# Attention output: rows loaded and stored by one transfer each, and weight blocks made in chosen slots

## The chip, the cores and the metric

The kernel runs on one core of one Trainium2 chip. The metric is device time in microseconds (us), from start to end of one execution; the median of several executions is compared. The core has a matrix engine (TensorE, PE in the profile, with its weight loads as PEld), three engines for elementwise work (VectorE = DVE, ScalarE = ACT, GpSimd = POOL), and SyncE (SP), which here does nothing but issue transfers (DMAs). All of them run their own instructions in order and wait for each other by semaphores. Transfers issued by any of them run on the core's 16 DMA engines.

## The reference

Two independent computations, put side by side in one output of 2048 rows and 2 x 576 columns.

```
A (attention):  q, k, v = x@wq, x@wk, x@wv        S = 2048 rows, D = 576, H = 32 heads of 18
  for each of 4 segments of 512 rows, for each head:
    p     = softmax(q k^T * scale + causal mask)
    a_mem = phi(q) M / (phi(q) z + 1e-6)           M, z: sums over earlier segments of phi(k)^T v, phi(k)
    o     = g * a_mem + (1 - g) * p v              g = sigmoid(beta), one number for each head
  out[:, :576] = concat_heads(o) @ wo
B (Fourier mixing):  out[:, 576:] = Cr @ (x @ Hr^T) - Ci @ (x @ Hi^T)     Cr, Ci: 2048 x 2048
```

Matrix products are made from numbers split into a high part (rounded to the matrix engine's float32 mode) and a low part (the rest): hi*hi + hi*lo + lo*hi.

## The kernel before, in words

**Stages.** First q, k, v and the memory of all segments are projected (up to some 225 us). Then the attention and the Fourier part B run interleaved (up to 938 us). Last stands the output stage, the product of the attention's result with `wo`.

**Attention.** `attention()` (L1110) is written as slots: 68 steps p of 8 slots each, one step for one pair of heads in one segment, with later work of earlier pairs in the same slots (scores for maxima in step p, second scores two and three steps later, the product with v four steps later: `F_LAG`, `T_LAG`, `V_LAG`). The main loop (L1181) takes one slot after the other, and behind each slot as many pieces of part B (`dense()`) as keep both at the same share of their work. `later(n, fn)` puts a call n slots ahead; transfers and low parts are mostly issued so. So the order on each engine is the order in which these lines run; no scheduler moves anything.

**The result on its way.** The normalised result of four heads is turned by VectorE (`turn_out`, L1081) and written to DRAM, to `od[s]`, four feature blocks of 128 x 512 rows for each segment s. Feature columns beyond 512 (64 of the 576) are gathered in `TAILS`, turned by `turn_tails` (L1096) and written to `odt[s]`, 256 rows of 128: twice for each segment, so eight times.

**The output stage.** The 16 tiles of 128 rows are taken as 8 pairs (tile n and tile n + 8), and each pair's product with `wo` is made by a Strassen-like scheme of seven products (`p1` to `p7` in `output_stage`, L849) in place of eight: rows in two halves (the two tiles), columns in two halves of 288, features in two halves of 256; features beyond 512 are added by `tail` terms. A product is 6 or 8 matmuls of 128 x 288 (`seventh`, L832), 50 for a pair. For this each pair's rows are loaded (`o_load`, `o_pair`, L684), split and combined into sums and differences (`left`, L789; the first pair's differences on VectorE, later ones on VectorE and GpSimd), two pairs ahead of their use at most. PSUM banks for the products alternate; `p6`, `p4` and `p7` of one pair share one bank, so `p7` waits until VectorE has emptied `p6` (L864).

Loading one tile takes three transfers: 128 x 4 x 128 from `od`, and twice 64 x 128 from `odt` (the same tail for the upper and the lower half of the partitions). Storing one tile takes four transfers of 32 rows (`store`, L843), because `turn_out` leaves the rows of a segment permuted in groups of 32. In the last pair some stores go on ScalarE's queue.

**Weight blocks.** `right_operands()` (L696) makes what the seven products need of `wo`: for each feature half c, the split blocks B11, B21, B22 (`plain`), the split differences T1 to T4 (`combined`, four differences of 128 x 288 in place, each using the one before, two on GpSimd and two on VectorE in turn, then high parts on ScalarE and low parts on VectorE), and the tail rows (`tails`). It is a generator: from step 60 on it goes one piece further at each slot, and at its end it loads the first pair (step 66) and goes on with `left(0)`. The second pair is loaded in the main loop's last part, once part B has no more chunks waiting.

Before, low parts of plain blocks are made by GpSimd, those of the tails by VectorE, those of the differences by VectorE.

**What sets the order of the transfers.** SyncE issues nearly all of them in program order; a transfer whose source or destination is not ready holds up those behind it. Completion is counted on eight counters that are used in turn, so a transfer also waits for the one that used its counter before.

Of the kernel before, what the change touches and what calls it, by code (L numbers as in the profile page):

```python
# [12 lines left out]
F32 = mybir.dt.float32  # L13
# [27 lines left out]
def infini_attention_and_fnet(ctx: ExitStack, tc: tile.TileContext, xT, wqk, w8, wv, wo, beta, xtT, cT, hT, out):  # L41
# [46 lines left out]
    def later(n, fn, *a):  # L88
        due.setdefault(clock[0] + n, []).append((fn, a))
# [54 lines left out]
    def wide_tile(cols):  # L144
        return lambda: wide.tile([P, cols], F32R, name="wide", tag="wide")
# [538 lines left out]
    def o_load(t, tile_of):  # L684
        s, a = divmod(t, 4)
        o = tile_of()
        dma(o[:, :4], od[s][:, a * P:a * P + P].rearrange("c p x -> p c x"))
        for i in range(2):
            dma(o[64 * i:64 * i + 64, 4], odt[s][64 * a:64 * a + 64])
        O[t] = o  # L690

    def o_pair(n):
        for t in (n, n + 8):
            o_load(t, lambda: sr.tile([P, 5, P], F32, name="craw", bufs=4))

    def right_operands():  # L696
        raw = {}
# [5 lines left out]
        def pause(n):  # L703
            for _ in range(n):
                yield

        def plain(c):
            b11 = wide.tile([P, 2, 288], F32R, name="wide", tag="wide")
            b2 = [wide_tile(D)() for _ in range(2)]
            WO["B11", c] = b11[:, 0], b11[:, 1]  # L710
            WO["B21", c], WO["B22", c] = ((b2[0][:, cs], b2[1][:, cs]) for cs in (slice(0, 288), slice(288, D)))
            for hi, lo, a in ((b11[:, 0], b11[:, 1], raw[c][:, :288]), (b2[0], b2[1], raw[c + 2])):
                act.activation(hi, a, AF.Copy)
                yield
                pool.tensor_tensor(lo, a, hi.bitcast(F32), OP.subtract)
                yield

        def cross(a, b, raw):
            act.activation(a, raw, AF.Copy)
            act.activation(b, raw, AF.Copy)  # L720
            yield
            dve.tensor_tensor(a[:64], raw[:64], a[:64].bitcast(F32), OP.subtract)
            dve.tensor_tensor(b[64:], raw[64:], b[64:].bitcast(F32), OP.subtract)
            yield

        def tails():
            w = [wide_tile(D)() for _ in range(2)]
            d = wide.tile([P, 2, 288], F32R, name="wide", tag="wide")
            TAIL[1], TAIL[2] = ([t[:, cs] for t in w] for cs in (slice(0, 288), slice(288, D)))
            TAIL[0] = [d[:, i] for i in range(2)]  # L730
            r = raw[4]
            yield from cross(*w, r)
            pool.tensor_tensor(r[:, :288], r[:, :288], r[:, 288:], OP.subtract)
            yield
            yield from cross(*TAIL[0], r[:, :288])
# [4 lines left out]
        spare = []  # L740

        def combined(c):
            a, b = raw.pop(c), raw.pop(c + 2)
            b11, b12, b21, b22 = a[:, :288], a[:, 288:], b[:, :288], b[:, 288:]
            if c == 0:
                spare.extend(stage(i, n) for i in range(2) for n in "qk")
                to = [[t[:, :D]] for t in spare]
            else:
                to = [[stage(2, n)[:, :D]] for n in "qk"] + [[wide_tile(D)()], [t[:, D:D + 288] for t in spare[:2]]]
            pool.tensor_tensor(b11, b12, b11, OP.subtract)  # L750
            yield
            dve.tensor_tensor(b12, b22, b12, OP.subtract)
            yield
            pool.tensor_tensor(b22, b22, b11, OP.subtract)
            yield
            dve.tensor_tensor(b21, b21, b22, OP.subtract)
            yield
            for names, r, hi, lo in ((("T1", "T3"), a, *to[:2]), (("T4", "T2"), b, *to[2:])):
                act.activation(hi[0], r, AF.Copy)
                yield  # L760
                at = 0
                for l in lo:
                    w = l.shape[1]
                    dve.tensor_tensor(l, r[:, at:at + w], hi[0][:, at:at + w].bitcast(F32), OP.subtract)
                    at += w
                for i, n in enumerate(names):
                    WO[n, c] = hi[0][:, 288 * i:288 * i + 288], lo[i] if len(lo) > 1 else lo[0][:, 288 * i:288 * i + 288]
                yield

        for k in (0, 2, 4):  # L770
            load(k)
            yield
        yield from pause(5)
        yield from plain(0)
        yield from tails()
        load(1)
        yield from pause(15)
        yield from combined(0)
        load(3)
        yield from pause(3)  # L780
        yield from plain(1)
        yield from combined(1)
        for t in (0, 8):
            o_load(t, lambda: sq.tile([P, 4, 256], F32, name="oraw", tag="qs3" if t else "ks3").rearrange(
                "p a x -> p (a x)")[:, :5 * P].rearrange("p (k x) -> p k x", k=5))
        yield from pause(4)
        yield from left(0)

    def left(n):  # L789
        one, two = O.pop(n), O.pop(n + 8)  # L790
# [50 lines left out]
            pe.matmul(o, a, b, start=first and i == 0, stop=True, skip_group_check=True)  # L841

    def store(t, y, cs, last=False):  # L843
        for q in range(4):
            r = 512 * (t // 4) + P * q + 32 * (t % 4)
            queue = nc.scalar if last and q >= 2 else nc.sync
            queue.dma_start(out[r:r + 32, cs], y[32 * q:32 * q + 32, cs])

    def output_stage():  # L849
        C, Z, U = slice(0, 288), slice(288, 576), {}  # L850
# [393 lines left out]
```

## Time and profile before

| | |
|---|---|
| median of 3 executions | 1009.91 us (1009.61 to 1010.26) |
| the profiled execution | 1010.71 us |
| its span, first to last instruction | 1009.0 us |
| granted TensorE clock, mean | 0.991 |
| TensorE busy | 984.3 us (98%) |
| VectorE, ScalarE, GpSimd busy | 786.2, 714.8, 675.6 us |
| transfers on SyncE's queue (q1) | 305248 packets, 207.15 MB |

In the profile's rows a group of instructions stands with its line, engine, operation and `out<-in` by the program's names, then count, busy time, mean duration in ns, and the idle time of the engine ahead of it with what ended it. Names that matter here: `raw` (rows of wo as loaded), `wide` and `late` (split weight blocks), `oraw`, `craw` (loaded rows of a pair; `craw` also holds part B's chunks), `ls`, `l`, `lb` (sums and parts of the first pair's rows), `u` (finished products, VectorE's and ScalarE's output), `d`, `s`, `t`, `pv` (PSUM banks), `ptt` (transposed probabilities), `og`, `ogt`, `oglt` (attention result and its turned forms). A stretch A:B is a piece of the span in us.

### The profile page before, as it was taken

What the parts mean: (1) busy time and instruction counts of PE and PEld (TensorE: products, weight loads), DVE (VectorE), ACT (ScalarE), POOL (GpSimd) and SP (SyncE); (2) the same over time, 40 slices, a digit from 0 to 9 for tenths busy, and PEclk for the clock granted to TensorE, in tenths of its full rate; (3) what the DMA queues carried; (4) which work ended last, traced back from release to release, by engine and by line L of the source; (5) the groups of instructions that cost most, each with busy time, mean ns of one, the idle gap of its engine ahead of it and who ended that gap; (6) DMA issues with size and microseconds to landing.
All of it is one profiled execution on the core that took longest, in us unless ns stands there. A gap on an engine that the chain in (4) does not pass through costs nothing.

```text
span 1009.0 us, 25590 instructions
## 1 busy us (share of the span) xinstructions
PE 984.3 (98%) x9246; PEld 921.7 (91%) x9246; DVE 786.2 (78%) x2112; ACT 714.8 (71%) x1686; POOL 675.6 (67%) x744
## 2 busy tenths in 40 slices
PE   9999999999999999999999999999999999998895
PEld 8989989899999999999999999999999999888895
DVE  6657667684778877878898887788889889988673
ACT  6757575754877878778878878877777777875341
POOL 2667575775767766766767777667766767786451
PEclk9999999999999999999999999999999999999898
DMA  7638466666778899899999988789999998896464
GB/s 242 198 121 262 149 202 243 216 236 210 170 192 200 235 235 222 210 223 253 224 250 225 223 203 174 185 228 211 244 227 214 238 226 230 218 207 146 124 161 107
DMA packets 305615, 208.92 MB, mean 207 GB/s; under 512 B 206288, under 2 KB 260432, under 8 KB 305488
## 3 DMA queue, kind: packets, MB, share of 16 engines
q1 hardware_dynamic: 305248, 207.15, 80.3%
q8 instruction: 72, 1.18, 0.5%
q14 instruction: 55, 0.45, 0.1%
q10 hardware_dynamic: 240, 0.14, 0.1%
HBM read 121.32 MB, written 57.93 MB: 178 GB/s over the span
## 4 chain that ended last, share of the span: by engine, by line
PE 77%; DVE 7%; ACT 4%; POOL 3%; issue 3%; DMA 3%; SPq 1%; POOLq 0%; DVEq 0%; ACTq 0%
PE d L583 35%; PE s L933 7%; PE v L84 4%; PE pv L1051 4%; PE qk L250 4%; PE d L630 3%; PE d L628 3%; PE d L629 3%; PE pv L1052 2%; DMA craw<-od 2%; PE m L363 1%; PE qk L84 1%; PE t L1007 1%; PE t L841 1%; DVE r L276 1%
## 5 line engine op out<-in xcount | busy, mean ns | idle before, releaser
L939 DVE CUSTOM_DVE_ANT_0 s<-s,causal 128x128 f32<-128x128 f32 (+3 forms) x512 | 248.5, 503 | 95.7 <-PE s L933 86.3
L456 POOL TENSOR_TENSOR clo<-craw,chi 128x512 fp32r<-128x512 f32 x158 | 219.7, 1391 | 88.6 <-ACT chi L451 61.8
L583 PE MATMUL d<-wide,chi 128*128 128x288 f32 x1408 | 263.2, 304 | 1.7 <-DVE y L653 1.7
L583 PEld LDWEIGHTS d<-wide,chi 128*128 128x128 f32 x1408 | 211.9, 190 | 4.2 <-DVE y L653 2.2
L583 PE MATMUL d<-wide,clo 128*128 128x288 f32 x704 | 174.1, 314 | 0.0
L973 POOL TENSOR_TENSOR hl<-pf,hl 128x768 f16<-128x768 f32 x64 | 114.0, 1781 | 68.7 <-ACT hl L969 57.2
L933 PE MATMUL s<-ks,qs 108*128 108x128 bf16 (+3 forms) x512 | 133.0, 303 | 2.9 <-DVE negm L939 1.2
L1019 ACT ACTIVATE phi<-t 128x384 f16<-128x384 f32 x128 | 61.7, 482 | 103.1 <-PE t L1016 103.1
L962 ACT ACTIVATE pf<-s,nb 128x128 f32<-128x128 f32 (+3 forms) x256 | 128.1, 526 | 6.2
L583 PE MATMUL d<-ab,chi 128*128 128x288 f32 x640 | 123.4, 302 | 0.0
L583 PEld LDWEIGHTS d<-wide,clo 128*128 128x128 f32 x704 | 118.5, 190 | 1.5
L1034 DVE TENSOR_TENSOR plo<-pf,phi 128x384 f16<-128x384 f32 (+1 forms) x128 | 118.6, 927 | 0.0
L1020 ACT ACTIVATE pf<-t 128x384 f32<-128x384 f32 (+1 forms) x192 | 99.5, 518 | 6.1 <-PE t L1007 5.7
L451 ACT ACTIVATE chi<-craw 128x512 fp32r<-128x512 f32 x160 | 100.1, 626 | 2.3 <-PE d L583 2.0
L583 PEld LDWEIGHTS d<-ab,chi 128*128 128x128 f32 x640 | 97.9, 189 | 0.5
L969 ACT ACTIVATE hl<-pf 128x768 f16<-128x768 f32 (+1 forms) x128 | 87.4, 730 | 2.0
L583 PE MATMUL d<-ab,clo 128*128 128x288 f32 x320 | 83.1, 309 | 0.0
L628 PE MATMUL d<-wide,chi 128*128 128x288 f32 x256 | 81.5, 318 | 0.0
L630 PE MATMUL d<-wide,clo 128*128 128x288 f32 x256 | 75.7, 296 | 0.9 <-POOL clo L456 0.9
L629 PE MATMUL d<-wide,chi 128*128 128x288 f32 x256 | 75.7, 296 | 0.0
L1034 POOL TENSOR_TENSOR plo<-pf,phi 128x384 f16<-128x384 f32 x64 | 61.8, 965 | 13.8 <-ACT pf L1020 11.0
L973 DVE TENSOR_TENSOR hl<-pf,hl 128x512 f16<-128x512 f32 x64 | 68.8, 1075 | 0.0
(279 smaller groups left out, 2531.4 us busy)
## 6 DMA issues: line engine op xcount, KB each, us to landing
craw<-cT SPq DMA_DIRECT2D x128, 256.0 KB
ks<-kd SPq DMA_DIRECT2D x32, 432.0 KB
qs<-qd SPq DMA_DIRECT2D x32, 432.0 KB
craw<-xtT SPq DMA_DIRECT2D x32, 320.0 KB
vd<-vs SPq DMA_DIRECT2D x16, 440.0 KB
vst<-vd SPq DMA_DIRECT2D x32, 220.0 KB
qd<-p SPq DMA_DIRECT2D x16, 384.0 KB
kd<-p SPq DMA_DIRECT2D x16, 384.0 KB
```

The costliest lines, as they stand in the source:

```text
L451: act.activation(hi, raw[:, :4], AF.Copy)
L456: engine.tensor_tensor(lo, raw[:, :4], hi.bitcast(F32), OP.subtract)
L583: pe.matmul(o[h], a, b[:, h * 288:h * 288 + 288], start=start, stop=stop)
L628: pe.matmul(o, xh[:, k], wl[k][:, cs], start=k == 0, stop=False)
L629: pe.matmul(o, xh[:, k], wh[k][:, cs], start=False, stop=False)
L630: pe.matmul(o, xl[:, k], wh[k][:, cs], start=False, stop=False)
L933: pe.matmul(o[:, c:c + w], q[:, i * P:w], k[:, :w], start=True, stop=True)
L939: dve.tensor_tensor_reduce(o[:, c:c + w], o[:, c:c + w], CAUSAL[0][:, L - w:], scale=scale, scalar=-LOWEST, op0=OP.add, op1=OP.min, accum_ ...
L962: act.activation(f[:, FIRST_COL[i]:FIRST_COL[i] + w], o[:, c:c + w], AF.Exp, bias=nb[:, i:i + 1], scale=-1.0)
L973: engine.tensor_tensor(hl[:, 1, a:b], f[:, a:b], hl[:, 0, a:b], OP.subtract)
L1020: act.activation(f[:, r:r + w], o[:, :w], AF.Exp, bias=LIFT, scale=SCALE)
L1034: (pool if kind == 2 else dve).tensor_tensor(lo[:, a:b], f[:, a:b], hi[:, a:b], OP.subtract)
```

## The change

1. `od[s]` gets a fifth block. When a segment's second tail write is out, three slots later one more transfer copies `odt[s]` into that block, each 64 rows twice (128 KB read, 256 KB written), four times in all. With it `o_load` is one transfer of 128 x 5 x 128.
2. `store` writes a tile with one transfer of 128 rows, the last tile's half with two of 64 rows, one on SyncE and one on ScalarE. The rows of columns 0 to 575 stay in the permuted order in the device's output; the caller puts them in order.
3. The second pair (tiles 1 and 9) is loaded in slot 4 of step 67, into the buffers `phi` and `plo` of the attention, in place of the load after the attention's end. The first pair is loaded in slot 5 of step 66 in place of slot 7.
4. `right_operands` is no generator any more: it writes a plan of calls, each at a step and slot. The plain blocks and tails begin at step 57 in place of 60. The low parts of the tails go from VectorE to GpSimd; the four differences that GpSimd made go to VectorE; the 576-column low parts of T1 to T4 become two of 288 each. For c = 0 the differences stand in step 64 and the low parts in step 65, for c = 1 in steps 66 and 67.
5. `left(0)` begins behind slot 5 of step 67 (before: behind slot 3).

TensorE's instructions and their order are the same in both.

```diff
-    od = [dram.tile([4, 4 * P, P], F32, name=f"od{s}") for s in range(NSEG)]
+    od = [dram.tile([5, 4 * P, P], F32, name=f"od{s}") for s in range(NSEG)]
...
-        dma(o[:, :4], od[s][:, a * P:a * P + P].rearrange("c p x -> p c x"))
-        for i in range(2):
-            dma(o[64 * i:64 * i + 64, 4], odt[s][64 * a:64 * a + 64])
+        dma(o, od[s][:, a * P:a * P + P].rearrange("c p x -> p c x"))
...
+        def at(p, slot, fn, *a):
+            PLAN.setdefault(8 * p + slot, []).append((fn, a))
...
+        def combined_low(c, n):
+            k, names = ((c, ("T1", "T3")), (c + 2, ("T4", "T2")))[n]
+            for i, x in enumerate(names):
+                low(dve, WO[x, c][1], WO[x, c][0], k, (L_, R_)[i])
...
+        at(57, 2, load, 0)
+        at(57, 4, load, 2)
+        at(58, 2, first_block, 0)
+        at(58, 2, second_row, 0)
+        at(58, 2, load, 4)
+        at(58, 4, block_low, 0)
+        at(59, 4, row_low, 0)
+        at(59, 2, tails)
+        at(60, 4, lambda: low(pool, late["w"][0], late["w"][0], 4, rows=lower))
+        at(61, 4, lambda: low(pool, late["w"][1], late["w"][1], 4, rows=upper))
+        at(61, 6, difference, pool, (4, L_), (4, L_), (4, R_))
+        at(62, 2, tail_difference)
+        at(62, 4, lambda: low(pool, TAIL[0][0], TAIL[0][0], 4, L_, lower))
+        at(62, 6, lambda: low(pool, TAIL[0][1], TAIL[0][1], 4, L_, upper))
+        at(62, 6, load, 1)
+        at(63, 6, first_block, 1)
+        at(64, 4, block_low, 1)
+        for c, p in ((0, 64), (1, 66)):
+            a, b = c, c + 2
+            if c:
+                at(65, 6, load, 3)
+                at(66, 2, second_row, 1)
+                at(66, 3, row_low, 1)
+            at(p, 3 + c, difference, dve, (a, L_), (a, R_), (a, L_))
+            at(p, 3 + c, difference, dve, (a, R_), (b, R_), (a, R_))
+            at(p, 5 + c, difference, dve, (b, R_), (b, R_), (a, L_))
+            at(p, 5 + c, difference, dve, (b, L_), (b, L_), (b, R_))
+            for n in range(2):
+                at(p + 1, 2, combined, c, n)
+                at(p + 1, 3 + n, combined_low, c, n)
         for t in (0, 8):
-            o_load(t, lambda: sq.tile(...tag="qs3" if t else "ks3")...)
-        yield from pause(4)
-        yield from left(0)
+            at(66, 5, o_load, t, lambda t=t: sq.tile(...tag="qs3" if t else "ks3")...)
+        for t, tag in ((1, "phi"), (9, "plo")):
+            at(67, 4, o_load, t, lambda tag=tag: sa.tile([P, 5, P], F32, name="oraw", tag=tag, bufs=2))
...
     def store(t, y, cs, last=False):
-        for q in range(4):
-            r = 512 * (t // 4) + P * q + 32 * (t % 4)
-            queue = nc.scalar if last and q >= 2 else nc.sync
-            queue.dma_start(out[r:r + 32, cs], y[32 * q:32 * q + 32, cs])
+        for q in range(2 if last else 1):
+            rows = slice(64 * q, 64 * q + 64) if last else slice(0, P)
+            (nc.scalar if q else nc.sync).dma_start(out[t * P:t * P + P][rows, cs], y[rows, cs])
...
+        if u:
+            later(6, dma, od[s][4].rearrange("(a c r) x -> a c (r x)", a=4, c=2),
+                  odt[s].rearrange("(a c r) x -> a c (r x)", a=4, c=1).to_broadcast([4, 2, 64 * P]))
...
-    ready = right_operands()
+    right_operands()
+    ready = None
     for n, w in enumerate(attention()):
         tick()
         ta += w
-        if n >= 8 * (NP - 4):
+        for fn, a in PLAN.pop(n, ()):
+            fn(*a)
+        if n == 8 * (NP + V_LAG - 1) + 5:
+            ready = left(0)
+        if ready:
             next(ready, None)
...
-        if not c_raw and 1 not in O:
-            o_pair(1)
```

More of the change, by code (lines that the diff above doesn't have):

```diff
@@ L701, in load @@
             dma(raw[k], wo[k])
[L703 to L724, printed above, removed]
-        def tails():
-            w = [wide_tile(D)() for _ in range(2)]
+        def high(o, k, cs=slice(0, D)):
+            act.activation(o, raw[k][:, cs], AF.Copy)
+        def low(engine, o, hi, k, cs=slice(0, D), rows=slice(0, P)):
+            engine.tensor_tensor(o[rows], raw[k][rows, cs], hi.bitcast(F32)[rows], OP.subtract)
@@ new lines, in right_operands, with first_block, second_row @@
+        L_, R_ = slice(0, 288), slice(288, D)
+        lower, upper = slice(0, 64), slice(64, P)
+        def first_block(c):
+            b = late["b", c] = wide.tile([P, 2, 288], F32R, name="wide", tag="wide")
+            WO["B11", c] = b[:, 0], b[:, 1]
+            high(b[:, 0], c, L_)
+        def second_row(c):
+            hi, lo = late["r", c] = [wide_tile(D)() for _ in range(2)]
+            WO["B21", c], WO["B22", c] = ((hi[:, cs], lo[:, cs]) for cs in (L_, R_))
+            high(hi, c + 2)
@@ L742, in combined @@
[L742 to L744 removed]
+        def combined(c, n):
+            k, names = ((c, ("T1", "T3")), (c + 2, ("T4", "T2")))[n]
             if c == 0:
[L746 to L768 removed]
@@ L770, in right_operands @@
[L770 to L782, printed above, removed]
+                hi, lo = late["s", n] = [stage(n, x) for x in "qk"]
+                lo = [lo[:, L_], lo[:, R_]]
+            elif n == 0:
+                hi, lo = [stage(2, x) for x in "qk"]
+                lo = [lo[:, L_], lo[:, R_]]
+            else:
+                hi, lo = wide_tile(D)(), [t[:, D:D + 288] for t in late["s", 0]]
```

34 lines of the change are left out of this document (24 added, 10 removed).

## The prediction

> **What bounds the kernel now.** I read the page first, then the stretches of its last 175 us, then the waits of TensorE there, then the instructions of VectorE and the DMA queue of SyncE in order of time. The page:
>
> ```profile
> span 1009.0 us, 25590 instructions
> PE 984.3 (98%) x9246; PEld 921.7 (91%) x9246; DVE 786.2 (78%) x2112; ACT 714.8 (71%) x1686; POOL 675.6 (67%) x744
> ```
>
> TensorE is the bound, and the change leaves its instructions and their order alone. What can move is the time in which it idles, the time in which it is clocked down, and what follows its last matmul. The stretches (time and count of PE, PEld, DVE, ACT, POOL, then granted clock, DMA share, GB/s):
>
> ```profile
> 750.00:800.00 50.00, 49.96 (x546) 46.86 (x544) 44.92 (x134) 37.20 (x88) 34.43 (x38) 1.00 0.97 230
> 835.00:880.00 45.00, 43.78 (x484) 40.98 (x483) 41.58 (x119) 35.08 (x82) 33.05 (x37) 1.00 0.87 221
> 880.00:930.00 50.00, 45.35 (x493) 42.98 (x490) 44.16 (x95) 36.00 (x83) 40.20 (x37) 1.00 0.86 192
> 929.50:933.50 4.00, 4.00 (x25) 3.93 (x21) 2.03 (x6) 1.67 (x5) 0.00 (x0) 0.57 0.00 0
> 945.40:950.80 5.40, 5.39 (x24) 5.39 (x25) 3.48 (x6) 2.19 (x4) 4.47 (x7) 0.54 0.51 138
> 956.00:980.00 24.00, 24.00 (x183) 24.00 (x183) 18.21 (x35) 11.23 (x30) 10.40 (x15) 1.00 0.60 158
> 980.00:999.40 19.40, 18.78 (x140) 18.32 (x138) 11.70 (x24) 5.99 (x13) 7.51 (x9) 1.00 0.52 132
> ```
>
> Up to 835 us there is nothing to gain. From 835 to 930 us TensorE idles 1.22 + 4.65 us. The granted clock is 0.57 for 4 us and 0.54 for 5.4 us, which costs 4.0 x 0.43 = 1.7 us and 5.4 x 0.46 = 2.5 us. TensorE's waits from 840 us on:
>
> ```profile
> PE t L841 <- DVE u L864: 5.1, 2, 4.6
> PE pv L1052 <- DVE plo L1034: 1.7, 2, 1.4
> PE d L583 <- DVE y L653: 1.7, 1, 1.7
> PE pv L1051 <- DVE og L1073: 1.3, 1, 1.3
> PE s L933 <- ACT pf L962: 1.2, 1, 1.2
> ```
>
> The longest stands at the opening of the output stage:
>
> ```profile
> 940.25 3.09 DMA craw<-od
> 943.43 0.42 DVE L812 TENSOR_TENSOR ls<-craw 128x256 f32<-128x256 f32 x1 [4.33 <-DMA craw<-od]
> 943.77 1.22 DVE L813 TENSOR_TENSOR wide<-craw,wide 128x512 fp32r<-128x512 f32 x1
> 944.91 0.45 DVE L864 TENSOR_TENSOR u<-t,u 128x288 f32<-128x288 f32 x1
> 945.41 1.81 PE L841 MATMUL t<-late,l 128*128 128x288 f32 x6 [4.55 <-DVE u L864]
> ```
>
> The second pair's rows land at 943.34. VectorE stands at L812 for them, and queued behind it is L864, which empties the bank that the next product needs: 4.55 us. After the last matmul the queue of SyncE sets the end:
>
> ```profile
> 976.92 3.78 SPq L847 DMA_DIRECT2D out<-u  x8
> 985.38 21.51 SPq L847 DMA_DIRECT2D out<-u  x34
> SPq L847 <- DMA out<-u: 4.9, 1, 4.9
> 995.69 11.20 SPq L847 DMA_DIRECT2D out<-u  x14
> 999.40 0.46 DVE L881 TENSOR_TENSOR u<-d,u 128x288 f32<-128x288 f32 x1 [0.61 <-PE d L841]
> 999.89 0.82 ACTq L847 DMA_DIRECT2D out<-u  x2
> 1001.42 0.80 SPq L847 DMA_DIRECT2D out<-u  x2
> ```
>
> The arithmetic is over at 999.86, the span at 1009.0: 9.14 us of stores. The two stores behind 995.69 are issued by 996.5; then SyncE waits 4.9 us for a store and issues the other twelve from 1001.42 to 1006.89, 0.46 us each. In the built program that waiting store shares its completion counter with ScalarE's first store, which goes out at 999.89 and lands 1.53 us later. So the stores of the seventh pair wait for the last result of the eighth.
>
> **The change part by part.** Sums are against the profiled execution, 1010.71 us with a span of 1009.0; the median of the runs is 1009.91, 0.8 less.
>
> *Stores, 68 to 18.* After the arithmetic one store is left to each queue (64 rows), and its counter is not shared with ScalarE's. SyncE ends its last issue 0.45 us after 999.86, and from there I take before's own end, 1009.0 - 1006.89 = 2.1 us: 2.6 us in place of 9.14, **-6.5 us**. The 128-row store just ahead of it has 288 KB to finish; the queue's row gives the rate (packets, MB, share of 16 engines):
>
> ```profile
> q1 hardware_dynamic: 305248, 207.15, 80.3%
> ```
>
> 207.15 MB in 80.3% of 16 x 1009 us is 16 KB/us an engine, 256 KB/us on 16, hence 1.1 us, of which part may show: -5.8 to -6.8.
>
> *Loads, six issues to two for each pair.* Between 980 and 999.4 TensorE idles 0.62 us. The last pair's loads are issued between the eight stores that end at 980.70 and those that begin at 985.38: six issues of 0.8 us, behind eight of 0.47. After, two behind two. **-0.6 us** (0 to -0.7).
>
> *Second pair's rows three slots sooner.* They go into buffers of the attention that are free by then, and SyncE asks for them right behind the first pair's, ahead of the last heads' two writes. Of these the first waits for the transposes at 937.11 (below), so that the loads are out before 937 and, at 3.09 us, landed by 940; the first pair's rows, next to them in the queue, are in use at 929.84. So the 4.33 us at L812 go. Late next is VectorE itself: the first pair's preparation starts two slots later than before, and half of it now falls behind the last heads' result. Rows of before for it:
>
> ```profile
> 929.84 0.69 DVE L813 TENSOR_TENSOR l<-oraw,l 128x512 fp32r<-128x512 f32 x1
> 935.64 0.30 DVE L1073 TENSOR_TENSOR og<-og,pv 128x144 f32<-128x144 f32 x1
> 937.11 0.51 DVE L1086 STREAM_TRANSPOSE ogt<-og 128x128 f32<-128x128 f32 x2
> 938.30 0.80 DVE L653 TENSOR_TENSOR y<-y,d 128x288 f32<-128x288 f32 x2
> 939.90 0.96 PE L841 MATMUL d<-late,l 128*128 128x288 f32 x6
> ```
>
> From 935.94, the end of L1073: three ops of 256 columns (0.42 each), transposes 0.51 and 0.27, two of L813's size (0.69), two short ones 0.49, two of y 0.80, some 4.5 us with their overlaps, until 940.4. Then L812 0.42, L813 0.69 to 1.22, L864 0.45: 942.0 to 942.5. TensorE is there at 940.86, so 1.1 to 1.7 us of the wait stay; I take 1.3 and book **-3.3 us** (-2.5 to -4.55). The low clock that follows cost 2.5 us. A stall of 1.6 us (1.3 and 0.3, below) was followed by the 0.57 stretch, 1.7 us; a stall of 1.3 may or may not cost that, so half of 1.7 stays: **-1.6 us** (0 to -2.5). The Trainium skill ("TensorE: Matmul & The Clock Gate", HAM oscillation) asks for idle gaps over about 3.4 us before the clock drops: by it the whole 2.5 us would go, and the sum be 0.9 us lower. The trace does not agree, for 0.57 follows stalls that add to 1.6 us.
>
> *Weight blocks in chosen slots.* VectorE's and GpSimd's rows of this work between 858 and 937 us:
>
> ```profile
> L752 DVE TENSOR_TENSOR raw<-raw 128x288 f32<-128x288 f32 x2 | 3.8, 1914 | 0.0
> L764 DVE TENSOR_TENSOR late<-raw,wide 128x288 fp32r<-128x288 f32 x2 | 3.0, 1540 | 0.0
> L723 DVE TENSOR_TENSOR wide<-raw,wide 64x576 fp32r<-64x576 f32 (+1 forms) x2 | 1.8, 913 | 0.1
> L722 DVE TENSOR_TENSOR wide<-raw,wide 64x576 fp32r<-64x576 f32 (+1 forms) x2 | 1.2, 594 | 0.0
> L756 DVE TENSOR_TENSOR raw<-raw 128x288 f32<-128x288 f32 x2 | 1.7, 866 | 1.4 <-POOL raw L754 1.4
> L715 POOL TENSOR_TENSOR wide<-raw,wide 128x288 fp32r<-128x288 f32 (+1 forms) x4 | 5.7, 1424 | 0.0
> L754 POOL TENSOR_TENSOR raw<-raw 128x288 f32<-128x288 f32 x2 | 2.4, 1212 | 0.4 <-DVE raw L752 0.4
> ```
>
> VectorE loses four tail ops (1.8 + 1.2 us) around 870 us and takes four differences from GpSimd (0.87 to 1.91 each, 3.5 to 7.6 us); its 1.4 us of waiting on GpSimd go, as no difference is passed between them any more. GpSimd loses those four (about 4 us at 880 to 920, where it is busy 40.2 of 50 us) and takes the tails: four ops of at most 1.4 to 1.8 us, about 6 us, into 850 to 880, where it has 12 us free; what it does late there delays the splits that TensorE reads two chunks later, and no wait on it is among the five rows. The five raw loads and the copies on ScalarE are the same in number and only move; where a load now waits for GpSimd's last tail or VectorE's last low part, the transposes behind it on SyncE are held up by about one such op, 1.4 us, within the nine slots until their use. Two stalls go with the old places: 1.7 (L653 behind the difference that waits for GpSimd) and 1.3 + 0.3 (behind two low parts of 1.54 that move past the last even head), with the 1.7 of clock: 5.0 us at most. Against that stand four low parts together in one head's third and fourth slots (3.5 to 6.2 us ahead of the minima) and the added differences. VectorE is at 44.16 of 50 us there, so I take half: **-2.5 us** (-5 to +3).
>
> *Four copies of the tails in DRAM*, 256 KB each, read from 128 KB: new, and no row shows one. Each follows every second write of such tails:
>
> ```profile
> L94 SPq DMA_DIRECT2D odt<-oglt x8: 326/385/454, 361.5 to 938.1; - x8
> ```
>
> Eight writes, 82 us apart, put the first three near 445, 610 and 775 us. Spread over 16 engines one holds each for 16 KB / 16 = 1 us; on one engine 256 / 16 = 16 us. It goes as eight pieces of 32 KB, so 2 us is nearest. Loads are asked for several slots ahead there and TensorE waits for none: **0** (0 to +12 for three). The last stands on SyncE ahead of the third pair's loads and waits for the write before it (1.5 us, as ScalarE's store above): these loads are issued by about 941.8 and land 3.1 us later, at 945; they are wanted at 945.6. **+0.5 us** (0 to +3). The Trainium skill ("DMA: Bandwidth & Descriptors", Rules for kernel authors) says an outermost dimension below 16 confines a transfer to that many engines; it is 4 on the source, so 64 KB an engine, an estimate of 4 us, and the third pair would be 2 us later, the sum about 1 us higher. No run here shows it yet.
>
> Sum: -6.5 - 0.6 - 3.3 - 1.6 - 2.5 + 0 + 0.5 = **-14.0 us**: 996.7 in the profiled execution's terms, 995.9 against the median. I say 996.
>
> **The rivals.**
> 1. *VectorE pays for the differences.* The blocks cost +3 instead of -2.5: 1001.5. For it: 44.16 of 50 us busy. Against it: its slow rows stand beside GpSimd's, which has less there. Chance 0.15.
> 2. *All stalls go.* With every idle and slow stretch gone (-6.8 - 0.7 - 4.55 - 2.5 - 5) it is 990.4. For it: at 24.00 us for 183 matmuls the output stage's 400 take 52.5 us, and they take 61.1 from 938.3 to 999.4. Against it: VectorE's 4.5 us behind the last heads. Chance 0.15. By the Trainium skill's clock rule above, a short wait at the opening would leave the clock alone.
> 3. *The early load does nothing*, because the last copy or VectorE's queue holds the opening as long as the late load did: without -3.3 and -1.6, 1001. Chance 0.08.
> 4. *Slower: the copies.* If each of the first three sits on few engines and the pieces of every later load on those queue behind it, TensorE starves near 445, 610 and 775 us. It decides from 14.0 / 3 = 4.7 us of starving each; at 16 us on one engine, less about 8 us of loads in hand, three give +24 - 14: 1020. Against it: SyncE's queue has slack of slots there, and TensorE's 49.96 of 50 us. Chance 0.05. By the Trainium skill's rule above, 4 us on four engines, it falls short of deciding: 1008 with no cover at all.
>
> **How the numbers follow.** Forecast 0.57, range 992 to 1001 from its terms. Case 1 and 3 end by 1003, case 2 by 989; the range 989 to 1003 leaves out case 4 and tails, about 0.15. Below the median by over 0.2% (2 us, about what a measurement of this kernel tells from no change): 0.93; within 0.01; slower 0.06.
>
> **What would show it.** Right: SyncE's last issue some 0.5 us behind the last VectorE op, 2.6 us to the end; no wait of VectorE for the second pair's rows and a wait of at most 2 us before the first seventh-product of bank t; no wait on GpSimd's differences. Wrong: TensorE's waits in the stretches behind 445, 610 or 775 us; a longer wait on minima or lows from 895 on; the output stage, 61.1 us now, above 58; VectorE waiting for the third pair's rows.

## The result and the profile after

The changed kernel takes 1000.40 us (median of 5 executions, 998.42 to 1001.23) against 1010.26 us (1009.61 to 1012.39) of the kernel before on the same chip: ratio 0.9891, 95% interval 0.9874 to 0.9909. It is faster by 1.1%, inside the range of 989 to 1003, and 4.4 us above the forecast of 996.0. The profiled execution took 998.66 us, 12.0 us less than the profiled one before; 14.0 were forecast in these terms. It is one of the quicker ones: the median lies 1.7 us above it after and 0.45 us below it before, so the medians show 9.9 us.

The page, the waits of TensorE from 840 us on, and the stretches of the end (columns as in the prediction):

```profile
span 997.0 us, 25491 instructions
PE 982.3 (99%) x9246; PEld 919.6 (92%) x9246; DVE 787.3 (79%) x2115; ACT 714.6 (72%) x1686; POOL 673.8 (68%) x744
```

```profile
PE pv L1066 <- ACT l L826: 2.1, 1, 2.1
PE t L857 <- DVE u L879: 1.9, 1, 1.9
PE pv L1067 <- DVE plo L1049: 1.6, 2, 1.2
PE d L583 <- DVE y L653: 0.6, 1, 0.6
```

```profile
835.00:880.00 45.00, 44.97 (x493) 42.16 (x493) 40.11 (x119) 35.25 (x83) 37.88 (x42) 1.00 0.98 237
926.00:930.00 4.00, 2.11 (x25) 2.02 (x26) 3.97 (x9) 1.30 (x5) 1.27 (x1) 0.74 0.62 173
930.00:936.00 6.00, 6.00 (x58) 5.93 (x58) 3.48 (x12) 0.64 (x1) 1.04 (x2) 0.89 0.00 0
942.00:948.00 6.00, 6.00 (x47) 6.00 (x46) 3.64 (x7) 2.16 (x6) 1.38 (x2) 1.00 0.85 230
980.00:993.00 13.00, 12.73 (x97) 12.50 (x95) 6.01 (x14) 1.61 (x4) 0.34 (x1) 1.00 0.27 103
```

The waits sum to 6.2 us where the five of before made 11.0. The stretch from 835 to 880 us has lost its idle time. The longest wait is now one that was not there: 2.1 us ahead of a product with v, at 926.7 us, and the clock is 0.74 and 0.89 behind it. The opening of the output stage waits 1.9 us instead of 4.55, and the clock behind it is 1.00 instead of 0.54.

The two ends of the output stage, in order of time: TensorE's first product in the kernel before, then, in the changed kernel, the same, VectorE at the opening, the wait of TensorE, and the last of VectorE and of ScalarE's queue:

```profile
938.32 0.96 PE L841 MATMUL s<-wide,l 128*128 128x288 f32 x6
```

```profile
937.28 0.96 PE L857 MATMUL s<-wide,l 128*128 128x288 f32 x6
939.62 0.45 DVE L653 TENSOR_TENSOR y<-y,d 128x288 f32<-128x288 f32 x1
939.98 0.42 DVE L828 TENSOR_TENSOR ls<-oraw 128x256 f32<-128x256 f32 x1
941.19 0.44 DVE L879 TENSOR_TENSOR u<-t,u 128x288 f32<-128x288 f32 x1
941.69 1.06 PE L857 MATMUL t<-late,l 128*128 128x288 f32 x6 [1.87 <-DVE u L879]
992.77 0.46 DVE L896 TENSOR_TENSOR u<-d,u 128x288 f32<-128x288 f32 x1 [0.61 <-PE d L857]
993.26 0.57 ACTq L862 DMA_DIRECT2D out<-u  x1
```

L828 no longer waits for the second pair's rows: it starts when VectorE has done with the last heads' `y`. The last result is there at 993.23, both queues have issued all by 993.83, and the span ends at 997.0. The 12.0 us divide by these rows into three: up to the first product of the output stage 938.32 - 937.28 = 1.0; from there to the last result 61.54 - 55.95 = 5.6; from the last result to the end 9.14 - 3.77 = 5.4.

### The profile page after: what moved, and what is told of

Its sections match the earlier page's. It is cut to its first block, busy times and chain, and to the rows that moved or that the text cites. A ratio compares the mean times of both kernels' runs of the same rounds, so it can differ in the third digit from the quotient of the medians.

```text
span 997.0 us, 25491 instructions
## 1 busy us (share of the span) xinstructions
PE 982.3 (99%) x9246; PEld 919.6 (92%) x9246; DVE 787.3 (79%) x2115; ACT 714.6 (72%) x1686; POOL 673.8 (68%) x744
## 4 chain that ended last, share of the span: by engine, by line
PE 84%; DVE 7%; ACT 4%; issue 2%; POOL 1%; DMA 1%; SPq 0%; POOLq 0%; DVEq 0%; ACTq 0%
PE d L583 37%; PE s L948 7%; PE v L84 4%; PE pv L1066 4%; PE qk L250 4%; PE d L630 3%; PE d L628 3%; PE d L629 3%; PE t L857 2%; PE pv L1067 2%; PE m L363 1%; PE d L857 1%; PE s L857 1%; PE t L1022 1%; PE qk L84 1%
## 5 line engine op out<-in xcount | busy, mean ns | idle before, releaser
L1049 DVE TENSOR_TENSOR plo<-pf,phi 128x384 f16<-128x384 f32 (+1 forms) x128 | 121.2, 947 | 0.0
```

Of the source, the lines that this page charges most:

```text
L1049: (pool if kind == 2 else dve).tensor_tensor(lo[:, a:b], f[:, a:b], hi[:, a:b], OP.subtract)
```

## The experiments

Ratios are against the kernel before on the same chip, with 95% intervals; the changed kernel's is 0.9891.

**1. The kernel before with the new stores alone.**

```diff
-        for q in range(4):
-            r = 512 * (t // 4) + P * q + 32 * (t % 4)
-            queue = nc.scalar if last and q >= 2 else nc.sync
-            queue.dma_start(out[r:r + 32, cs], y[32 * q:32 * q + 32, cs])
+        for q in range(2 if last else 1):
+            rows = slice(64 * q, 64 * q + 64) if last else slice(0, P)
+            (nc.scalar if q else nc.sync).dma_start(out[t * P:t * P + P][rows, cs], y[rows, cs])
```

> The kernel before with only the stores changed (one transfer for a tile, two for the last tile's half). Theory: the 9.14 us behind the last VectorE instruction become some 3.8 us as in the changed kernel, and nothing else moves but the last pair's loads: 5.4 to 6 us below the kernel before, a ratio of 0.994 to 0.9946, and the profile's opening wait of TensorE stays at about 4.5 us. Rival (the stores were hidden, and the whole gain comes from the opening): within 1 us of the kernel before.

Measured: 1003.54 us (1002.79 to 1004.52), ratio 0.9935 [0.9922, 0.9948], 6.5 us off the median, a little more than the 5.4 to 6 expected. The last of VectorE:

```profile
997.63 0.46 DVE L880 TENSOR_TENSOR u<-d,u 128x288 f32<-128x288 f32 x1 [0.61 <-PE d L841]
```

With a span of 1001.4 the end after the last result is 3.3 us in place of 9.14: 5.8 of the gain. The profiled execution is 7.6 us below the one before; most of the rest is 1.7 us of clock near 930 us, which the stores do not touch (last section). The opening wait of TensorE stays at 4.5 us, as expected. So the stores alone give about half of the 12.0 us between the profiles; by the medians it is 6.5 of 9.9.

**2. The kernel before, its 68 stores kept, the last ones all on SyncE.**

```diff
-            queue = nc.scalar if last and q >= 2 else nc.sync
+            queue = nc.sync
```

> The kernel before with all its 68 small stores, but the last eight all on SyncE, so that no store of SyncE shares a counter with one of ScalarE. Theory (two causes, the wait on the shared counter and the number of issues): the 4.9 us wait of SyncE goes, the issues stay; from 996.5 fourteen issues of 0.46 us, held up by their data now and then, end near 1003, and 2.1 us more make 1005: 3 to 4.5 us below the kernel before. Rival A (the number of issues alone is the cause): the two more issues on SyncE cost 0.9 us and the time is 0 to 1 us above the kernel before. Rival B (the counter alone): 6 us below, as with the large stores.

Measured: 1006.22 us (1005.45 to 1007.73), ratio 0.9962 [0.9948, 0.9975], 3.8 us off. In its trace SyncE's wait of 4.9 us for a store is gone. So 3.8 us of the old end were that wait, through a counter shared with ScalarE's queue. The other 2.7 of experiment 1 are put down to the number of issues, as the difference of two medians. The profiles give nearly the same split without the clock: the time behind the last result is 9.14 us before, 5.4 here and 3.3 in experiment 1, so 3.7 for the wait and 2.1 for the issues.

**3. The changed kernel with the second pair loaded late again.**

```diff
-        for t, tag in ((1, "phi"), (9, "plo")):
-            at(67, 4, o_load, t, lambda tag=tag: sa.tile([P, 5, P], F32, name="oraw", tag=tag, bufs=2))
...
+        if not c_raw and 1 not in O:
+            o_pair(1)
```

> The changed kernel with the second pair loaded as in the kernel before, behind the attention, by two transfers into craw buffers. Theory: VectorE waits for the rows again, TensorE's wait at the opening grows from 1.9 us to some 4 to 5 us and the clock drops behind it: 3 to 6 us above the changed kernel. Rival (the opening is bound by VectorE's own queue, the early load does nothing): within 1 us of the changed kernel.

Measured: 1006.84 us (1006.10 to 1009.94), ratio 0.9966 [0.9957, 0.9975]. Its opening:

```profile
PE t L855 <- DVE u L877: 8.5, 1, 8.5
```

```profile
946.87 0.98 DVE L826 TENSOR_TENSOR ls<-craw 128x256 f32<-128x256 f32 x1 [6.80 <-DMA craw<-od]
```

The early load is worth 6.4 us by the medians, above the expected range, as the late load in this kernel waits 8.5 us where it waited 4.55 before. The rows now stand behind the last copy: they are asked for at 939.84 us, 0.8 us after it, and used 7.0 us later. So the 6.4 us are the price of a late load in the changed kernel, not what the early load saved against the kernel before. Experiments 7 to 9 return to the copy.

**4. The changed kernel with the weight blocks made as before** (the generator of before in place of the plan; the rest stays).

```diff
-    def right_operands():
-        raw, late = {}, {}
...
+    def right_operands():
+        raw = {}
...
-    right_operands()
+    rows_plan()
+    blocks = right_operands()
...
+        if n >= 8 * (NP - 4):
+            next(blocks, None)
```

> The changed kernel with the weight blocks made as in the kernel before (generator from step 60 on, tails' low parts on VectorE, half of the differences on GpSimd); stores, loads and the first pair's preparation as in the changed kernel. Theory: the waits of TensorE at 874, 906, 921 and 928 us return in place of those at 901, 906, 926 and 928, some 1.5 to 3 us above the changed kernel. Rival (the new places cost VectorE as much as they save): within 1 us. Rival 1 of the prediction (VectorE pays for the differences): 2 to 5 us below the changed kernel.

Measured: 1000.20 us (998.35 to 1003.50), ratio 0.9904 [0.9888, 0.9920]. Of TensorE's waits from 840 us on:

```profile
PE d L583 <- DVE y L653: 1.7, 1, 1.7
PE pv L1054 <- DVE og L1076: 1.3, 1, 1.3
PE s L936 <- ACT pf L965: 1.2, 1, 1.2
```

By medians the new places give nothing (-0.2 us), by ratios 1.3 us with an uncertainty of 2.4. The old waits of 1.7, 1.3 and 1.2 are back, and the 2.1 is gone: the plan trades 4.2 us of waits for 2.7 (the 2.1 and the 0.6 that is left of the 1.7). In the profiles the product at the opening starts at 942.84 us here and at 941.69 in the changed kernel, 1.15 us apart, behind the same wait of 1.87. Most of the rest of the difference between the two spans (999.8 and 997.0) is 1.7 us of clock behind that wait, which was lost here and not there (last section).

**5. The changed kernel with half of the c = 1 differences later.**

```diff
-            at(p, 5 + c, difference, dve, (b, R_), (b, R_), (a, L_))
-            at(p, 5 + c, difference, dve, (b, L_), (b, L_), (b, R_))
+            at(*((67, 2) if c else (p, 5)), difference, dve, (b, R_), (b, R_), (a, L_))
+            at(*((67, 2) if c else (p, 5)), difference, dve, (b, L_), (b, L_), (b, R_))
...
-                at(p + 1, 2, combined, c, n)
-                at(p + 1, 3 + n, combined_low, c, n)
+                at(p + 1, 3 if c and n else 2, combined, c, n)
+                at(p + 1, 4 if c and n else 3 + n, combined_low, c, n)
```

> The changed kernel with the second two of the four differences of c = 1 moved from step 66 slot 6 to step 67 slot 2, the high part made from them to slot 3 and its low parts to slot 4. Theory (the 2.1 us wait of TensorE at 926.7 us is VectorE's: four differences of 1.4 to 1.6 us each stand ahead of the minima and of the result of pair 66; the next wait of 1.2 us at 928.1 and the slow clock behind them follow from it): both waits shrink to below 1 us each, the clock stays at 1.00 from 926 to 936 us, and the time falls by 2 to 4 us to 996.5 to 998.5. Rival (VectorE's total work in the last two steps is what counts, wherever it stands): the wait moves to the last head or to the opening of the output stage, and the time stays within 1 us of 1000.4.

Measured: 995.91 us (994.88 to 996.97), ratio 0.9852 [0.9835, 0.9869]: 4.5 us below the changed kernel by the medians, 3.9 by the ratios. VectorE around the place, first in the changed kernel, with the product of TensorE that waited, then here; then the stretches here:

```profile
922.81 2.03 DVE L739 TENSOR_TENSOR raw<-raw 128x288 f32<-128x288 f32 x2
926.20 0.30 DVE L1088 TENSOR_TENSOR og<-og,pv 128x144 f32<-128x144 f32 x1
926.65 0.19 PE L1066 MATMUL pv<-vst,phi 128*128 128x55 bf16 x1 [2.10 <-ACT l L826]
```

```profile
924.49 0.30 DVE L1088 TENSOR_TENSOR og<-og,pv 128x144 f32<-128x144 f32 x1
925.98 0.94 DVE L739 TENSOR_TENSOR raw<-raw 128x288 f32<-128x288 f32 x2
```

```profile
926.00:930.00 4.00, 3.88 (x60) 3.82 (x61) 3.92 (x11) 1.92 (x5) 0.00 (x0) 1.00 0.66 186
930.00:936.00 6.00, 6.00 (x47) 6.00 (x47) 5.80 (x16) 2.87 (x8) 3.16 (x5) 1.00 0.10 33
```

With two differences fewer ahead of it, the result of the heads before (L1088) ends 1.7 us sooner, the 2.1 us wait is gone and the clock stays at 1.00. The profile had put that wait down to ScalarE's L826. Here L826 runs from 927.54 to 928.16, and the same product (L1066) starts at 924.94 without it, so it was not that one. It was L1088: the product starts 0.15 us after L1088 ends, in the changed kernel (926.50, 926.65), here (924.79, 924.94), in experiment 7 (929.95, 930.10) and, at L1073, in the kernel before (928.31, 928.46), where the profile names it. The gain is a little more than the 2 to 4 us expected. The two differences themselves take 0.94 us here and took 2.03 there, where GpSimd's `clo` ran beside them.

**6. Four copies where there was one**, behind each of the first three segments (three more, into buffers that nothing reads).

```diff
+            if s < 3:
+                for x in odx[s]:
+                    later(6, dma, x.rearrange("(a c r) x -> a c (r x)", a=4, c=2),
+                          odt[s].rearrange("(a c r) x -> a c (r x)", a=4, c=1).to_broadcast([4, 2, 64 * P]))
```

> The changed kernel with three more copies of the tails behind each of the first three segments' copies (into DRAM buffers that nothing reads): four in a row where there was one, 9 more in all. Theory (the copies lie beside loads that are asked for early enough, and cost nothing): within 2 us of the changed kernel's 1000.4, no wait of TensorE near 445, 610 and 775 us, and the rows of the copies show how long one takes. Rival (a copy sits on few engines and holds the loads behind it, only just covered by the slack of slots): four in a row eat the slack, TensorE waits for loads at those places, 4 us or more at each, 12 us or more in all.

Measured: 1016.73 us (1014.99 to 1019.52), ratio 1.0065 [1.0049, 1.0082], 16 us above the changed kernel. The rival held in all and at two of the three places. The longest wait of TensorE and three stretches here, then two of them in the changed kernel:

```profile
PE t L1023 <- DMA qs<-mt: 8.7, 2, 4.4
```

```profile
448.00:472.00 24.00, 19.58 (x204) 18.12 (x200) 14.92 (x45) 14.50 (x34) 13.04 (x12) 0.93 0.91 196
618.00:642.00 24.00, 22.38 (x237) 21.16 (x236) 18.39 (x57) 16.24 (x44) 15.78 (x21) 1.00 0.87 175
788.00:818.00 30.00, 25.66 (x250) 23.81 (x249) 20.60 (x63) 17.86 (x41) 18.46 (x19) 0.89 0.94 212
```

```profile
448.00:472.00 24.00, 23.95 (x266) 22.53 (x264) 19.07 (x58) 19.92 (x48) 15.96 (x18) 1.00 1.10 234
788.00:818.00 30.00, 29.85 (x317) 28.00 (x316) 26.66 (x80) 22.31 (x52) 19.94 (x22) 1.00 0.95 243
```

TensorE idles 8.6 us more in the first and the third stretch, and the clock loses 24 x 0.07 + 30 x 0.11 = 5.0 more there, 13.6 of the 16. At both places it waits for transfers of 3 KB (`qs<-mt`) that were issued behind the copies. At the first the copies' packets run from 455.99 to 466.26 us, four at a time, and the wait ends at 466.65. At the middle place TensorE idles only 1.6 us, behind ScalarE, which waits 3.4 us for a load. One copy at each place is covered; four are not. Two and three were not tried.

**7. The changed kernel with the first pair prepared sooner.**

```diff
-        if n == 8 * (NP + V_LAG - 1) + 5:
+        if n == 8 * (NP + V_LAG - 1) + 3:
```

> The changed kernel with one edit: left(0) begins behind slot 3 of step 67, as before the change, in place of slot 5. Theory (the 1.87 us that TensorE still waits at the opening of the output stage is VectorE's queue, in which the first pair's preparation starts two slots later than before): the opening wait shrinks to 0.5 to 1.2 us and the time falls by 0 to 1.2 us against the changed kernel's 1000.4. Rival (VectorE's work ahead of the minima of the last heads is what counts, and preparation two slots sooner pushes it back): the opening wait falls, but a wait of 1 us or more comes up between 926 and 937 us, and the time is the same or up to 2 us longer.

Measured: 1002.11 us (1000.15 to 1006.02), ratio 0.9917 [0.9898, 0.9936], not told apart from the changed kernel. The profiled execution is the slowest of the six. Its opening wait went to 0.19 us, below the expected 0.5 to 1.2; but in neither expectation stood what came instead:

```profile
944.44 1.05 PE L857 MATMUL t<-late,l 128*128 128x288 f32 x6 [0.19 <-DVE u L879]
954.43 1.81 PE L857 MATMUL t<-late,wide 128*128 128x288 f32 x6 [3.09 <-DVE u L879]
```

A wait of 3.09 us stands one pair later, for the third pair's rows.

**8. Both edits (5 and 7), and then the same without the copies.** The second kernel loads a tile by three transfers, as before the change:

```diff
-        dma(o, od[s][:, a * P:a * P + P].rearrange("c p x -> p c x"))
+        dma(o[:, :4], od[s][:4, a * P:a * P + P].rearrange("c p x -> p c x"))
+        for i in range(2):
+            dma(o[64 * i:64 * i + 64, 4], odt[s][64 * a:64 * a + 64])
...
-        if u:
-            later(6, dma, od[s][4].rearrange("(a c r) x -> a c (r x)", a=4, c=2),
-                  odt[s].rearrange("(a c r) x -> a c (r x)", a=4, c=1).to_broadcast([4, 2, 64 * P]))
```

> Both edits together: the second two differences of c = 1 and what is made of them later (step 67, slots 2 to 4), and left(0) behind slot 3. Theory (each wait has its own place in VectorE's queue): the gains add, 995.5 to 998. Rival (VectorE is full from 918 to 940 us, so whatever is put off is paid at the opening): the opening wait is 2 us or more and the time is 999 to 1001.

> The kernel with late differences and left(0) behind slot 3 (999.18), but with loads of three transfers and no copies. Theory (its 3.02 us wait of TensorE at 947 us is the copy's: the third pair's rows, asked for at 937.74 behind the copy, land at 945.44, 7.7 us later): without the copy they land by 942, the 3.02 us wait falls below 1 us, and the time falls by 2.5 to 5 us to 994 to 996.7. Rival (the loads are late since the transposes of the last heads stand behind the preparation in VectorE's queue, copy or not): the wait stays at 2 us or more, 998.5 to 1000.

Measured: with copies 999.18 us (998.73 to 999.93), ratio 0.9885 [0.9869, 0.9902]; without 993.89 us (993.29 to 994.51), ratio 0.9835 [0.9820, 0.9849]. The first took the rival's time, but not by its way: the opening wait is 1.24 us, and a longer one comes behind it. SyncE, VectorE and TensorE in order of time, and a stretch, of the first; then SyncE and VectorE of the second, and its only wait in the output stage:

```profile
936.46 0.70 SPq L94 DMA_DIRECT2D od<-odt  x1
937.74 5.09 SPq L687 DMA_DIRECT2D craw<-od  x4
945.44 0.42 DVE L828 TENSOR_TENSOR ls<-craw 128x256 f32<-128x256 f32 x1 [4.42 <-DMA craw<-od]
947.42 1.35 PE L857 MATMUL t<-late,wide 128*128 128x288 f32 x6 [3.02 <-DVE u L879]
```

```profile
948.00:952.00 4.00, 4.00 (x21) 4.00 (x20) 3.29 (x7) 1.67 (x4) 3.74 (x5) 0.57 0.55 186
```

```profile
935.78 0.39 SPq L687 DMA_DIRECT2D craw<-od  x1
941.77 0.42 DVE L830 TENSOR_TENSOR ls<-craw 128x256 f32<-128x256 f32 x1 [1.31 <-DMA craw<-od]
```

```profile
PE t L859 <- DVE u L881: 1.2, 1, 1.2
```

The two gains do not add while the copy is there. Without it the third pair's rows are asked for 1.96 us sooner (935.78 against 937.74) and used 6.0 us after that in place of 7.7; the 3.02 us wait is gone, and with it 4 x 0.43 = 1.7 us of slow clock. The two kernels differ in the copies and in the form of the loads, but the form alone is not it. In the changed kernel and in that of experiment 5 a tile also takes one transfer, and the copy goes out 2.45 us ahead of the loads instead of 1.28; there the rows are used 5.9 and 6.05 us after they are asked for. By the medians this is the fastest kernel of the study, 16.4 us below the one before; the last of experiment 10 can't be told from it.

**9. The changed kernel without the copies**, with loads of three transfers (the second diff of experiment 8 alone).

> The changed kernel with its loads of token rows as before the change (three transfers for a tile, the tails straight from odt) and without the four copies. Theory (as predicted: one transfer in place of three is worth 0.6 us in the output stage, the copies cost 0 to 0.5 us): 999.5 to 1001, within 1 us of the changed kernel's 1000.4. Rival (the copies cost something in the changed kernel after all, since one copy holds the DMA engines it sits on for some 5 us): 996 to 999.

Measured: 998.30 us (997.74 to 1000.81), ratio 0.9883 [0.9865, 0.9901]. The median lies in the rival's range, but by the ratios it is 0.8 us with an uncertainty of 2.5 and can't be told from the changed kernel: the one-transfer loads with their copies bring nothing there that shows.

**10. VectorE empties the bank first**, in the kernel of experiment 5, and the same without the copies.

```diff
                 piece = fn(k)
                 next(piece)
+                if n == 0:
+                    next(piece, None)
                 next(prepare, None)
                 next(piece, None)
```

> The kernel with late differences (995.91), and in the first pair's products VectorE empties the bank ahead of the second pair's preparation (L828, L829: 1.36 us) instead of behind it. Theory (the opening wait of 1.87 us is VectorE's queue): the wait shrinks to 0.5 to 0.8 us and the time to 994.4 to 995.3. Rival (the preparation that is put back is itself late next): a wait of 1 us or more comes up between 940 and 950 us, and the time is 995.5 to 998.

> The kernel with late differences and the bank emptied first, but with loads of three transfers and no copies. Theory (in it nothing waits for the copy, as VectorE's wait for the third pair's rows is not passed on to TensorE): within 1 us of the kernel with the bank emptied first. Rival (the copy delays the third pair's rows enough that TensorE comes to wait for them once VectorE is sooner): 1.5 to 3 us faster than that kernel.

Measured: 995.57 us (994.96 to 995.95), ratio 0.9852 [0.9835, 0.9868], as fast as the kernel that it starts from; without copies 994.50 us (994.36 to 994.81), ratio 0.9841 [0.9827, 0.9856]. TensorE at the waits, with copies and without:

```profile
936.82 1.07 PE L857 MATMUL t<-late,l 128*128 128x288 f32 x6 [0.67 <-DVE u L879]
945.04 1.06 PE L857 MATMUL t<-late,wide 128*128 128x288 f32 x6 [1.31 <-DVE u L879]
```

```profile
936.94 1.05 PE L859 MATMUL t<-late,l 128*128 128x288 f32 x6 [0.74 <-DVE u L881]
944.59 1.06 PE L859 MATMUL t<-late,wide 128*128 128x288 f32 x6 [0.75 <-DVE u L881]
```

The opening wait shrank from 1.87 to 0.67 us, and 1.31 came up behind it for the third pair's rows, as the rival had it. Without copies that wait is 0.75, and the time 1.1 us less: between the two expectations.

## Why the prediction was right, and where it was off

**Stores, -6.5: right in kind; the end is 1.1 us longer than forecast.** Experiments 1 and 2 show both parts, the shared counter (3.7 us by the profiles) and the number of issues (2.1). Behind the last issue I took before's 2.1 us; it is 997.0 - 993.8 = 3.2. SyncE's last waits for a store, before and after:

```profile
SPq L1239 <- DMA out<-u: 1.0, 1, 1.0
```

```profile
SPq L1260 <- DMA out<-u: 1.7, 2, 1.5
```

The step that failed is taking the end behind a store of 32 rows for that behind one of 64. It accounts for about half: in experiment 2, with stores of 32 rows, the end is again 2.1 us, and in experiment 1, where only the stores changed, it is 2.7, with waits of 1.7 as here. The other half is not in the stores: the three kernels without copies end in 2.7 us, those with copies in 2.8 to 3.4. Its cause was not tried.

**Loads, -0.6: the time came, but from the stores.** The 0.62 us of idle time at the end of the output stage are gone; the 0.27 us in the stretch from 980 to 993 are time behind the last product, which ends at 992.74. But in experiment 1, whose loads still take six issues for a pair, TensorE is busy 19.59 of the 19.60 us up to its last product. The new stores alone free those loads, so the step that failed is booking the time to fewer load issues. Experiment 9 agrees.

**Second pair sooner, -3.3 and -1.6: right, -4.9 against 2.7 + 2.5 = 5.2 by the rows.** The way was as forecast: no wait of VectorE for these rows, `y` done at 940.07 (forecast: the backlog until 940.4), then L828, L829 and the emptying of the bank, 941.63 (forecast 942.0 to 942.5, with a stage that began 1.0 us later). The wait that is left is 1.87, a little above 1.1 to 1.7. Its low clock did not come at all, where I had left half. That is luck: in experiments 4 and 6 the same wait of 1.87 us was followed by a clock that cost 1.7 us (last section). The third rival (the early load does nothing) falls by experiment 3.

**Weight blocks, -2.5: mis-sized.** The trace gives 1.0 us up to the output stage, the profile of experiment 4 1.15. The step that failed is "two stalls go with the old places: 5.0 us at most", of which I took half. They go but for 0.6 us, and the four differences on VectorE become the next wait. The group by lines shows the price: eight of them at 1.14 us, within the 0.87 to 1.91 that I gave.

```profile
L739 DVE TENSOR_TENSOR raw<-raw 128x288 f32<-128x288 f32 x8 | 9.1, 1138 | 0.1
```

So the price was right. What I did not do is put the differences into VectorE's queue ahead of the last but one result (L1088), for which TensorE waits. That is the first rival's mechanism at a smaller size, and experiment 5 gets 4 us back from it.

**Copies, 0 and +0.5: right for the first three; the last is hidden by VectorE.** The stretches near 450 and 800 us show no idle time of TensorE above 0.15 us, and near 620 there is none, so the fourth rival did not come; experiment 6 shows that its mechanism is real: four in a row cost 16 us. Of the last copy, 1.15 us from 939.3 on hold nothing else (queue, packets, MB, share of 16 engines):

```profile
q1 hardware_dynamic: 4, 0.13, 45.8%
```

Four packets of 32 KB, half of the copy, at 0.458 x 16 x 1.15 / 4 = 2.1 us each. "It goes as eight pieces of 32 KB, so 2 us is nearest" took the eight at once; four go at a time: the other four start at 941.6, when the first end, and take 1.3 us each, so the copy runs from 939.56 to 943.08, 3.5 us. The Trainium skill ("DMA: Bandwidth & Descriptors", Rules for kernel authors), which confines the copy to four engines, would make that two rounds, an estimate of about 4 us; the trace agrees. It costs nothing here since VectorE reaches the third pair's rows late: it waits 1.3 us for them and TensorE does not. With VectorE sooner and the copy closer to the loads it is the next wait, 3.0 to 3.1 us (experiments 7 and 8).

**The second rival, all stalls go (990.4),** did not come, but most of the way to it can be gone: experiment 8 stands at 993.9.

In sum -12.0 against -14.0: 1.1 from the end of the stores, 1.5 from the weight blocks, against 0.6 better in the output stage, which rests on the clock that happened to hold. The other 2.4 us of the miss lie between the profiled executions and the medians: the runs after spread from 998.42 to 1001.23 with the granted clock from 0.998 down to 0.995. In size that is the spread (0.003 x 997 = 3.0 us), and it would fit the slow clock behind the waits that are left; but only one of the five was profiled, so where the others lost it is not shown. The four runs of experiment 5 have 0.999 each.

## What to carry to other kernels

Moving work to a busy in-order engine is sized from its queue, not from the sum: list what stands behind each moved instruction, up to the next result that TensorE waits for. When a wait goes, look which transfer or result is next in line, since here each was 1 to 3 us behind the other (second pair's rows, VectorE's preparation, third pair's rows behind the copy). At the end of a kernel look at which queues share a completion counter before counting bytes.

## What the runs showed of the hardware

*The same short waits are followed by different clocks.* The waits at 921 and 928 us (1.7 and 1.3 us) were followed by different clocks in the kernel before and in experiment 1 (where all is 0.9 us later), whose code is the same up to there:

```profile
929.00:935.00 6.00, 6.00 (x64) 5.93 (x65) 3.11 (x9) 2.08 (x5) 0.00 (x0) 0.72 0.00 0
```

```profile
929.00:935.00 6.00, 5.29 (x70) 5.14 (x71) 4.51 (x12) 2.63 (x6) 0.00 (x0) 1.00 0.08 24
```

That is 1.7 us in one profile and none in the other, so a clock loss that one profile shows is not a fixed price. The single wait of 1.87 us at the opening is followed by a clock of 1.00 in the changed kernel and in experiments 5 and 9. In experiment 4 the same wait, which ends at 942.84, is followed by this:

```profile
945.00:950.00 5.00, 5.00 (x32) 5.00 (x32) 3.77 (x7) 2.04 (x6) 2.01 (x2) 0.79 0.73 192
```

Over 943 to 949 us that is a clock of 0.72, which costs 1.7 us; experiment 6 has the same behind its opening, 0.72 over 6 us. The wait of 3.02 us in experiment 8 cost 1.7 us too. What decides is not shown. The Trainium skill ("TensorE: Matmul & The Clock Gate", HAM oscillation) asks for gaps over about 3.4 us; the waits of 1.87 and 3.02 us are below that and the clock dropped, so the measurement decides against it.

*A few large packets hold small ones.* Transfers of 3 KB behind four 256 KB copies kept TensorE waiting 4.4 us (experiment 6); the mean share of the DMA engines was 0.91 there, against 1.10 with one copy, so the load on all 16 does not show it.
